# The first batch of a Fourier-mixing and gated-MLP kernel: another row order, another cut of its first stage, another layout of its spills

## The chip, the cores and the metric

The kernel runs on one core of one Trainium2 chip. The metric is the device time of one launch in microseconds, from the first instruction to the last. The kernel before takes 1937.45 us (median of 3 runs, 1937.38 to 1937.58). TensorE (PE) runs the matmuls, from tiles of up to 128 partitions in SBUF into tiles of 512 float32 values per partition in PSUM (a "bank" in the code). VectorE (DVE), ScalarE (ACT) and GpSimd (POOL) do the rest. Transfers run on 16 DMA engines and are issued here from two queues, SyncE's (SP) and ScalarE's.

## The reference

```python
def _attn_ref(x):                       # x: 8 batches x 3008 rows x 256, float32
    X = np.fft.fft(x, axis=1)
    X = np.fft.fft(X, axis=2)
    return X.real.astype(np.float32)

def _moe_ref(x, w_in, w_out):           # x: 24064 x 256, w_in 256 x 2048, w_out 2048 x 256
    h = x @ w_in
    g = h * (1.0 / (1.0 + np.exp(-1.702 * h)))
    return (g @ w_out).astype(np.float32)

out = _moe_ref(_attn_ref(x).reshape(24064, 256), w_in, w_out)
```

The kernel works in float32. It writes the 3008-point transform as 47 x 64: row s of a batch is 64 p + j. A first stage sums over the 47 values of p, for each j, with a matrix of sines and cosines; a second stage sums over j. By symmetry, j and 64 - j are taken together, and so are columns d and 256 - d (the "fold"). The weights arrive as 64-bit words and are turned into float32 by a chain of bit operations ("rounding", in 4 pieces each of w_in and w_out).

## The kernel before

Only the start of the program is touched, and the spill of every batch. The first batch is loaded into `xt` with the rows of j = 0 to 31 on partitions 0 to 46 and those of 64 - j on partitions 47 to 93, so that one matmul over 94 partitions (128 with zeros) sums both; the later batches come by `load_x`, another way, which is not touched.

```python
NA, NB = 47, 64
NJ = NB // 2
NM = 48
ENDS = 0, NJ, NJ + 1, NJ + 2
PIECES = (0, 32), (32, NA)
NU, NG = 2, 12

    ...

    def load_first(lo, hi, engines):
        for p0, p1 in PIECES:
            n, src = p1 - p0, NB * p0 * D
            engines[0].dma_start(out=xt[p0:p1, lo:hi, :].rearrange("p j d -> p (j d)"),
                                 in_=view(x, src + lo * D, [NB * D, n], [1, (hi - lo) * D]))
            t, a = xt[NA + p0:NA + p1], max(lo, 1)
            if lo == 0:
                engines[1].dma_start(out=t[:, 0, :], in_=view(x, src + NJ * D, [NB * D, n], [1, D]))
            engines[1].dma_start(out=t[:, a:hi, :], in_=view(x, src + (NB - a) * D, [NB * D, n], [-D, hi - a], [1, D]))

    def fold_first(k):
        t, e = xt[0:2 * NA, 4 * k:4 * k + 4, :], room[k % 4][0:2 * NA]
        nc.scalar.copy(free(e, 0, [D, 4], [H, 2]), free(t, 0, [D, 4], [H, 2]))
        for at, op in ((1, ALU.add), (H + 1, ALU.subtract)):
            nc.vector.tensor_tensor(e[:, :, at:at + H - 1], t[:, :, 1:H], free(t, D - 1, [D, 4], [-1, H - 1]), op=op)

    def mix_first(k):
        ps, e = bank("ps1"), room[k % 4]
        for r in range(2):
            for even in range(2):
                for c in range(2):
                    jj, (c0, c1) = 4 * k + 2 * r + c, (0, H + 1) if even else (H + 1, D)
                    w, n = (w0o, jj) if jj and not even else (w0, jj or ENDS[1 - even])
                    nc.tensor.matmul(ps[64 * c:64 * c + 64, r * D + c0:r * D + c1], lhsT=mat(w, n, slice(0, 128)),
                                     rhs=e[:, 2 * r + c, c0:c1], start=True, stop=True)
        nc.scalar.copy(xt[:, 2 * k:2 * k + 2, :].rearrange("p j d -> p (j d)"), ps[:])

    def warm(n):
        ps = bank("warm")
        for _ in range(n):
            nc.tensor.matmul(ps[:], lhsT=wcs[0][:, 0:128], rhs=wcs[0][:, 0:512], start=True, stop=True)

    def spill(b, q0=0, q1=16, engines=(nc.sync, nc.sync)):
        for c, eng in enumerate(engines):
            eng.dma_start(out=view(Td[b], (2 * q0 + c) * D, [NJ * D, NM], [2 * D, q1 - q0], [1, D]),
                          in_=xt[64 * c:64 * c + NM, q0:q1, :])

    def fill(b, a0=0, a1=NG):
        if a0 == 0:
            t4t[b] = tp.tile([128, NG, D], F32, tag="t4", name="t4")
        nc.sync.dma_start(out=t4t[b][:, a0:a1, :], in_=Td[b].rearrange("(a p) d -> p a d", p=128)[:, a0:a1, :])

    def rotate(b, a0=0, a1=NG, copy=None):
        col = t4t[b][:, a0:a1, H]
        ps = bank("psr")
        nc.tensor.matmul(ps[:, 0:a1 - a0], lhsT=rot, rhs=col, start=True, stop=True)
        (copy or nc.vector.tensor_copy)(col, ps[:, 0:a1 - a0])

    ...

    def bounds(key, low=None):
        hi, lo = raw[key][:, :, 1].bitcast(F32), raw[key][:, :, 0]
        g = sp.tile([128, 1024], F32, tag="s", bufs=3, name="g")
        m = cv.tile([128, 1024], F32, tag="m", name="m")
        r = cv.tile([128, 1024], U32, tag="r", bufs=2, name="r")
        nc.scalar.activation(g[:], hi, ACTF.Square)
        nc.gpsimd.tensor_scalar(m[:], hi, scalar1=TOP, scalar2=-TOP, op0=ALU.min, op1=ALU.max)
        ...                                  # (a variant that nothing calls)
        else:
            nc.scalar.activation(r[:].bitcast(F32), lo, ACTF.Copy, scale=2.0 ** -29, bias=2.0 ** 23)
            nc.scalar.activation(r[:], r[:].bitcast(F32), ACTF.Copy, bias=-2.0 ** 23)
        pre[key] = g, m, r

    def rounded(outs, key):
        raw.pop(key)
        g, m, r = pre.pop(key)
        ...
        dve.scalar_tensor_tensor(m[:], g[:], LOW * LOW, m[:], op0=ALU.is_ge, op1=ALU.mult)
        dve.tensor_scalar(a[:], bits, scalar1=3, scalar2=0x3FFFFFF8, op0=ALU.logical_shift_left, op1=ALU.bitwise_and)
        dve.scalar_tensor_tensor(a[:], bits, 0xC0000000, a[:], op0=ALU.bitwise_and, op1=ALU.bitwise_or)
        def finish():
            for out, part in outs(a[:], r[:]):
                nc.gpsimd.tensor_tensor(out.bitcast(U32), *part, op=ALU.add)
        return finish

    ...

    def fold_w(n):
        for cs in range(2):
            ps = bank("psw")
            for i in range(2):
                nc.tensor.matmul(ps[:], lhsT=cd[:, i, cs, :], rhs=wst[n][:, i, :], start=(i == 0), stop=(i == 1))
            nc.scalar.copy(wcs[cs][:, n * 512:(n + 1) * 512].rearrange("p (f c) -> p f c", f=4),
                           free(ps[:], 0, [1, 4], [4, 128]))
        row = cv.tile([1, 512], F32, tag="e", name="row")
        nc.scalar.activation(row[:], ps[0:1, :], ACTF.Copy, scale=2.0)
        nc.scalar.dma_start(out=af2[:, 4 * n:4 * n + 4], in_=row[:])

    ... (program order of the start; the loop over the steps of all batches follows)

    n0 = (NJ + 1) * NM + 64 - NM
    w0 = wt[:].rearrange("p a q n -> p (a q n)")[:, 0:n0 + 1]
    w0o = wt[:].rearrange("p a q n -> p (a q n)")[:, 2048:2048 + n0]
    room += [hp.tile([128, 4, D], F32, tag="h", name="e") for _ in range(4)]
    nc.vector.memset(wcs[0][:, 0:512], 1.0)
    for e in room:
        nc.gpsimd.memset(e[64:128], 0.0)
    nc.vector.memset(ones[:], 1.0)
    nc.scalar.dma_start(out=w0, in_=tab1[:, 0:n0 + 1])
    both = nc.sync, nc.scalar
    load_first(0, 8, (nc.sync, nc.sync))
    load_first(8, 20, both)
    load_first(20, 32, both)
    nc.scalar.dma_start(out=small[:], in_=tab2)
    load_in(0, nc.sync)
    load_in(1, nc.sync)
    load_out(0, nc.sync)
    warm(6)
    nc.vector.tensor_scalar(w0o, w0[:, 0:n0], scalar1=w0[:, n0:n0 + 1], scalar2=None, op0=ALU.mult)
    fold_first(0)
    for k in range(8):
        if k < 7:
            fold_first(k + 1)
        mix_first(k)
        if k in (3, 5, 7):
            spill(0, 0 if k == 3 else 2 * k - 2, 2 * k + 2, both if k == 7 else (nc.sync, nc.sync))
    fill(0, 0, 4)
    bounds(("in", 0))
    round_in(0)
    finish_in(0)
    warm(4)
    bounds(("in", 1))
    fold_w(0)
    fill(0, 4, NG)
    load_out(1, nc.sync)
    rotate(0, 0, 4, nc.scalar.copy)
    stage2(0, 0)
    round_in(1)
    finish_in(1)
    bounds(("out", 0))
    load_in(2, nc.sync)
```

So each group k of the first stage takes four values of j (`xt[:, 4k:4k+4]`), folds their rows with one ScalarE copy and two VectorE operations into `e`, runs 8 matmuls in pairs (the two `c` write different halves of the output's partitions) into one PSUM bank, and copies that bank back to `xt`. `spill` writes the result to device memory, `fill` reads it back in another order, `rotate` and `stage2` (32 matmuls of 64 x 32 each way, and a VectorE transpose) follow. Every matmul in float32 is two records in the trace. `fold_w` multiplies a rounded piece of w_in with a matrix; `hidden`, the step's first matmuls (pa and pb in the trace, L422), needs both this and stage 2. After that the program is a loop of 384 steps over all batches, with the remaining rounding of the weights among its first.

## Time and profile before

| what | value |
|---|---|
| time | 1937.45 us |
| span of the profiled execution | 1934.7 us |
| TensorE busy | 1903.0 us of it (98%) |
| VectorE, ScalarE, GpSimd busy | 1405.5, 673.3, 761.0 us |
| mean DMA rate | 53 GB/s |
| TensorE busy in the first 31 us, the next 8, the next 10.3 | 18.77, 3.59, 7.79 us (warm-up matmuls included) |
| TensorE busy from 90 to 1900 us | 1810.00 of 1810 us |

The page gives busy time of each engine as a share of the span. TensorE is busy almost throughout, and the idle time it has lies at the start and in the last microseconds. So the time is the length of the start, up to where the matmul stream begins, plus that stream. Which of the waits at the start ends last is read from the chain of waits and the timeline, not from the shares. "PEclk" in the tables of windows is the clock that TensorE was granted, 1.00 being the full one.

### The profile page before, as it was taken

How to read it: one execution, taken by the hardware profiler on the slowest of the kernel's cores; microseconds unless marked ns; L12 is line 12 of the kernel's file. 1: busy time of each engine (PE TensorE's matmuls, PEld its weight loads, DVE VectorE, ACT ScalarE, POOL GpSimd, SP SyncE). 2: the span in 40 equal slices, each digit the busy share in tenths (PEclk: the TensorE clock that was granted, in tenths of full speed). 3: DMA queues.
4: the chain of work that ended last, by engine and by line, in shares of the span. 5: the costliest groups of instructions: out<-in, count | busy, mean ns of one | idle time of the engine just before them, and what ended most of it. 6: DMA issues, size and time to landing. Idle time of an engine off the chain costs nothing.

```text
span 1934.7 us, 29225 instructions
## 1 busy us (share of the span) xinstructions
PE 1903.0 (98%) x10690; PEld 1667.3 (86%) x10690; DVE 1405.5 (73%) x2924; ACT 673.3 (35%) x927; POOL 761.0 (39%) x1049
## 2 busy tenths in 40 slices
PE   6899999999999999999999999999999999999998
PEld 3598888988889888898889888898888988889887
DVE  3877777777778677876777677777777777777776
ACT  3733333333333333333333333333333333333332
POOL 2565323643246322462235523255323643223222
PEclk8999999999999999999999999999999999999999
DMA  9630460227203362025422162221720213202201
GB/s 249 168 70 11 94 80 12 49 54 113 17 12 59 49 108 18 21 49 97 61 25 49 29 106 39 25 49 43 115 25 13 18 45 59 17 12 27 17 12 22
DMA packets 157652, 103.40 MB, mean 53 GB/s; under 512 B 105403, under 2 KB 142011, under 8 KB 156857
## 3 DMA queue, kind: packets, MB, share of 16 engines
q1 hardware_dynamic: 154160, 98.70, 30.4%
q10 hardware_dynamic: 3350, 2.84, 0.7%
q8 instruction: 85, 1.39, 0.3%
q14 instruction: 57, 0.47, 0.1%
HBM read 58.24 MB, written 48.01 MB: 55 GB/s over the span
## 4 chain that ended last, share of the span: by engine, by line
PE 96%; DMA 1%; POOL 1%; issue 1%; DVE 1%; ACT 0%; ACTq 0%; SPq 0%; DVEq 0%; POOLq 0%
PE po L489 59%; PE pa L422 17%; PE pb L422 17%; PE ps L205 1%; PE ps L287 1%; DMA xt<-in_x_dram 1%; PE psw L392 1%; PE ps L244 0%; POOL wo L354 0%; PE ps L209 0%; POOL wst L354 0%; POOL m L330 0%; DVE a L350 0%; DVE m L347 0%; DVE os L506 0%
## 5 line engine op out<-in xcount | busy, mean ns | idle before, releaser
L463 POOL TENSOR_TENSOR s<-h 128x256 f32<-128x256 f32 (+1 forms) x376 | 270.3, 719 | 1092.0 <-ACT h L451 1027.6
L489 PE MATMUL po<-s,wt 128*128 128x256 f32 (+1 forms) x2256 | 599.7, 375 | 0.0
L426 ACT COPY v<-pa 128x512 f32<-128x512 f32 (+1 forms) x384 | 222.0, 578 | 1061.8 <-PE pa L422 1061.8
L436 DVE TENSOR_TENSOR h<-v,pb 128x512 f32<-128x512 f32 (+1 forms) x384 | 259.0, 675 | 401.5 <-PE pb L422 398.7
L489 PEld LDWEIGHTS po<-s,wt 128*128 128x128 f32 x2256 | 428.6, 190 | 48.4
L489 PE MATMUL po<-h,wo 128*128 128x256 f32 (+1 forms) x1632 | 469.7, 375 | 0.5 <-ACT h L451 0.5
L451 ACT ACTIVATE h<-h 128x1024 f32<-128x1024 f32 (+1 forms) x384 | 400.8, 1044 | 18.9 <-DVE h L446 16.7
L422 PE MATMUL pa<-pq,wcs 128*128 128x256 f32 (+1 forms) x1536 | 393.7, 379 | 1.3 <-DVE pq L293 1.3
L422 PE MATMUL pb<-pq,wcs 128*128 128x256 f32 (+1 forms) x1536 | 387.9, 375 | 2.2 <-DVE dif L439 1.6
L489 PEld LDWEIGHTS po<-h,wo 128*128 128x128 f32 x1632 | 309.9, 190 | 36.4 <-issue 0.8
L422 PEld LDWEIGHTS pa<-pq,wcs 128*128 128x128 f32 x1536 | 286.8, 190 | 49.6 <-issue 11.2
L439 DVE SCALAR_TENSOR_TENSOR dif<-nb,af,pb 128x256 f32<-128x256 f32 (+1 forms) x768 | 328.3, 469 | 1.7 <-DMA af<-row 1.7
L422 PEld LDWEIGHTS pb<-pq,wcs 128*128 128x128 f32 x1536 | 291.5, 190 | 36.4 <-DVE dif L439 2.0
L464 POOL TENSOR_TENSOR s<-h 128x256 f32<-128x256 f32 (+1 forms) x376 | 276.9, 736 | 0.0
L446 DVE TENSOR_TENSOR h<-pa,dif 128x512 f32<-128x512 f32 (+1 forms) x448 | 265.4, 604 | 13.2
L489 PE MATMUL po<-h,wt 128*128 128x256 f32 (+1 forms) x752 | 220.3, 375 | 0.0
L489 PE MATMUL po<-s,wo 128*128 128x256 f32 (+1 forms) x752 | 220.3, 375 | 0.0
L467 DVE TENSOR_TENSOR s<-h,s 128x256 f32<-128x256 f32 (+1 forms) x376 | 201.2, 535 | 12.9
L466 DVE TENSOR_TENSOR s<-s,h 128x256 f32<-128x256 f32 (+1 forms) x376 | 179.5, 477 | 4.3 <-POOL s L463 4.3
L489 PEld LDWEIGHTS po<-h,wt 128*128 128x128 f32 x752 | 142.9, 190 | 16.1
L489 PEld LDWEIGHTS po<-s,wo 128*128 128x128 f32 x752 | 142.9, 190 | 16.1
L191 POOL TENSOR_TENSOR xt<-xt 111x510 f32<-111x510 f32 x56 | 74.1, 1323 | 4.4
(60 smaller groups left out, 691.8 us busy)
## 6 DMA issues: line engine op xcount, KB each, us to landing
out_dram<-os SPq DMA_DIRECT2D x284, 64.0 KB
Td<-xt SPq DMA_DIRECT2D x14, 768.0 KB
t<-Td SPq DMA_DIRECT2D x7, 1536.0 KB
xt<-in_x_dram SPq DMA_DIRECT2D x14, 512.0 KB
xt<-Xr SPq DMA_DIRECT2D x14, 512.0 KB
nb<-pq SPq DMA_DIRECT2D x23, 256.0 KB
out_dram<-os SPq DMA_DIRECT2D x96, 56.0 KB
Xr<-in_x_dram SPq DMA_DIRECT2D x7, 752.0 KB
```

Of the source, the lines that this page charges most:

```text
L191: eng.tensor_tensor(low, low, free(t, up + D - 1, [-D, 2], [-1, D - 1]), op=ALU.add)
L422: nc.tensor.matmul(ps[:, i * 256:i * 256 + n], lhsT=wcs[cs][:, f * 128:(f + 1) * 128], rhs=pq[:, cs, ks], start=True, stop=True)
L426: nc.scalar.copy(two(v[:], n), two(pa[:], n))
L436: nc.vector.tensor_tensor(two(h[:], n), two(v[:], n), two(pb[:], n), op=ALU.add)
L439: nc.vector.scalar_tensor_tensor(dif[:, i * 256:i * 256 + n], nb[:, ks], af2[:, f:f + 1], pb[:, i * 256:i * 256 + n], op0=ALU.mult, op1=AL ...
L446: nc.vector.tensor_tensor(free(h[:], 512 + at + m - 1, [256, 2], [RUN, blocks], [-1, m]), *ins, op=ALU.add)
L451: nc.scalar.activation(g, g, ACTF.Gelu_apprx_sigmoid)
L463: eng.tensor_tensor(s1, a21, a22, op=ALU.add)
L464: eng.tensor_tensor(s3, a11, a21, op=ALU.subtract)
L466: eng.tensor_tensor(s2, s1, a11, op=ALU.subtract)
L467: eng.tensor_tensor(s4, a12, s2, op=ALU.subtract)
L489: nc.tensor.matmul(pot[q][:, i, :n], lhsT=lhs, rhs=rhs, start=(p == 0 and i == 0 and f == 0), stop=(p == NP - 1), skip_group_check=True)
```

## The change

The first batch is laid out by halves: partitions 0 to 63 hold the rows of j = 0 to 31 in their natural order, partitions 64 to 127 the rows of j = 32 to 63, again in natural order, no longer reversed. Each half is loaded as rows 0 to 31 and rows 15 to 46, 32 partitions each (rows 15 to 31 twice; the matrix has zeros for the second copy). A partition then receives one contiguous run of 8 KB per load, where the reversed rows came in runs of 1 KB. As 64 - j now lies in another slot than j, the two halves can't be summed in one matmul: each product is taken over 64 partitions, and the halves are added in PSUM. Groups k and 7 - k are computed together, in two phases, so that at any time the lower half of the array adds to one bank and the upper half to the other. Between the phases two ScalarE copies of one column hold the second phase back until the first is through. The matmuls double in number and use a quarter of the array each. The columns of the second stage are permuted in the tables, so that a spill writes long runs: 16 KB per partition for the later batches, 4 KB and 2 KB for the first, against 1 KB. The order of the loads, the number of warm-up matmuls, the place of one weight load (`load_out(0)`) and the engines of a few early operations change too (cuts are marked "...", empty lines left out).

```diff
--- before.py
+++ after.py
@@ -71,13 +71,17 @@
     e0, o0, e1, o1 = ENDS
     w1[:, e0, :, 0], w1[:, o0, :, 0], w1[:, e1, :, 1], w1[:, o1, :, 1] = cos[:, 0], sin[:, 0], cos[:, NJ], sin[:, NJ]
-    w0 = np.zeros((128, NJ + 1, NG * NU, 2))
-    w0[:NA], up = w1[:, :NJ + 1], w0[NA:2 * NA]
+    up = np.zeros_like(w1[:, :NJ + 1])
     up[:, 1:NJ, :, 0], up[:, 1:NJ, :, 1] = cos[:, :NJ:-1], -sin[:, :NJ:-1]
     up[:, e0, :, 1], up[:, o0, :, 1] = cos[:, NJ], sin[:, NJ]
-    sign = np.where((np.arange(128) < NA) | (np.arange(128) >= 2 * NA), 1.0, -1.0)
-    j, k2 = np.arange(NJ)[:, None], np.arange(NB)[None, :]
+    w0 = np.zeros((2, 64, NJ + 1, NG * NU, 2))
+    for half, w in enumerate((w1[:, :NJ + 1], up)):
+        w0[half, :32], w0[half, 64 - (NA - 32):] = w[:32], w[32:]
+    sign = np.repeat([1.0, -1.0], 64)
+    c, q = np.divmod(np.arange(NJ), 16)
+    j, k2 = (4 * (q // 2) + 2 * (q % 2) + c)[:, None], np.arange(NB)[None, :]
     beta = 2.0 * np.pi * ((j * k2) % NB) / NB
     m2 = np.zeros((NU, 2, NJ, 2, NB))
     rot = np.zeros((NU, 2, NJ, NU, 2, NJ))
@@ -145,6 +149,7 @@
     def bank(name):
         return psm.tile([128, 512], F32, tag="mm", name=name)
@@ -214,36 +219,52 @@
-    room = []
+    room = {}
     def load_first(lo, hi, engines):
-        for p0, p1 in PIECES:
-            n, src = p1 - p0, NB * p0 * D
-            engines[0].dma_start(out=xt[p0:p1, lo:hi, :].rearrange("p j d -> p (j d)"),
-                                 in_=view(x, src + lo * D, [NB * D, n], [1, (hi - lo) * D]))
-            t, a = xt[NA + p0:NA + p1], max(lo, 1)
-            if lo == 0:
-                engines[1].dma_start(out=t[:, 0, :], in_=view(x, src + NJ * D, [NB * D, n], [1, D]))
-            engines[1].dma_start(out=t[:, a:hi, :], in_=view(x, src + (NB - a) * D, [NB * D, n], [-D, hi - a], [1, D]))
-    def fold_first(k):
-        t, e = xt[0:2 * NA, 4 * k:4 * k + 4, :], room[k % 4][0:2 * NA]
+        for half in range(2):
+            for g in range(2):
+                eng, p = engines[2 * half + g], 64 * half + 32 * g
+                eng.dma_start(out=xt[p:p + 32, lo:hi, :].rearrange("p j d -> p (j d)"),
+                              in_=view(x, (NB * (NA - 32) * g + NJ * half + lo) * D, [NB * D, 32], [1, (hi - lo) * D]))
+    def fold_first(g):
+        t, e = xt[:, 4 * g:4 * g + 4, :], room[g]
         nc.scalar.copy(free(e, 0, [D, 4], [H, 2]), free(t, 0, [D, 4], [H, 2]))
         for at, op in ((1, ALU.add), (H + 1, ALU.subtract)):
             nc.vector.tensor_tensor(e[:, :, at:at + H - 1], t[:, :, 1:H], free(t, D - 1, [D, 4], [-1, H - 1]), op=op)
     def mix_first(k):
-        ps, e = bank("ps1"), room[k % 4]
-        for r in range(2):
-            for even in range(2):
-                for c in range(2):
-                    jj, (c0, c1) = 4 * k + 2 * r + c, (0, H + 1) if even else (H + 1, D)
-                    w, n = (w0o, jj) if jj and not even else (w0, jj or ENDS[1 - even])
-                    nc.tensor.matmul(ps[64 * c:64 * c + 64, r * D + c0:r * D + c1], lhsT=mat(w, n, slice(0, 128)),
-                                     rhs=e[:, 2 * r + c, c0:c1], start=True, stop=True)
-        nc.scalar.copy(xt[:, 2 * k:2 * k + 2, :].rearrange("p j d -> p (j d)"), ps[:])
+        ks = k, 7 - k
+        ps = [bank("ps1") for _ in ks]
+        for phase in range(2):
+            if phase:
+                for n in range(2):
+                    nc.scalar.copy(af2[:, n:n + 1], ps[n][:, D + n * (H + 1):D + n * (H + 1) + 1])
+            for at in range(4)[::-1 if phase else 1]:
+                r, even = divmod(at, 2)
+                for half in (phase, 1 - phase):
+                    n = half ^ phase
+                    for c in range(2):
+                        jj = 4 * ks[n] + 2 * r + c
+                        c0, c1 = (0, H + 1) if even ^ half ^ phase else (H + 1, D)
+                        slot, first = ((NB - jj) % NJ if half else jj), c0 == 0
+                        w, m = (w0o, jj) if jj and not first else (w0, jj or ENDS[1 - first])
+                        rows_ = slice(64 * half, 64 * half + 64)
+                        nc.tensor.matmul(ps[n][64 * c:64 * c + 64, r * D + c0:r * D + c1], lhsT=mat(w, m, rows_),
+                                         rhs=room[slot // 4][rows_, slot % 4, c0:c1], start=(phase == 0 and at == 0),
+                                         stop=(phase == 1), skip_group_check=True)
+        for n in range(2):
+            to = placed(ks[n])
+            nc.scalar.copy(xt[:, to:to + 2, :].rearrange("p j d -> p (j d)"), ps[n][:])
+    def placed(k):
+        return 2 * k if k < 4 else 16 + 2 * k
     def load_matrices():
         for r in range(2):
@@ -256,11 +277,17 @@
         for _ in range(n):
             nc.tensor.matmul(ps[:], lhsT=wcs[0][:, 0:128], rhs=wcs[0][:, 0:512], start=True, stop=True)
-    def spill(b, q0=0, q1=16, engines=(nc.sync, nc.sync)):
+    def spill(b, ks=None, engines=(nc.sync, nc.sync)):
         for c, eng in enumerate(engines):
-            eng.dma_start(out=view(Td[b], (2 * q0 + c) * D, [NJ * D, NM], [2 * D, q1 - q0], [1, D]),
-                          in_=xt[64 * c:64 * c + NM, q0:q1, :])
+            src, at = xt[64 * c:64 * c + NM], 16 * c * D
+            if ks is None:
+                eng.dma_start(out=view(Td[b], at, [NJ * D, NM], [1, 16 * D]),
+                              in_=src[:, 0:16, :].rearrange("p q d -> p (q d)"))
+                continue
+            (k0, n), k1 = ks, 8 - sum(ks)
+            eng.dma_start(out=view(Td[b], at + 2 * k0 * D, [NJ * D, NM], [2 * (k1 - k0) * D, 2], [1, 2 * n * D]),
+                          in_=free(src, placed(k0) * D, [(placed(k1) - placed(k0)) * D, 2], [1, 2 * n * D]))
     def fill(b, a0=0, a1=NG):
         if a0 == 0:
@@ -319,22 +346,21 @@
     pre = {}
-    def bounds(key, low=None):
+    def bounds(key, first=False):
         hi, lo = raw[key][:, :, 1].bitcast(F32), raw[key][:, :, 0]
         g = sp.tile([128, 1024], F32, tag="s", bufs=3, name="g")
         m = cv.tile([128, 1024], F32, tag="m", name="m")
         r = cv.tile([128, 1024], U32, tag="r", bufs=2, name="r")
-        nc.scalar.activation(g[:], hi, ACTF.Square)
+        if first:
+            nc.vector.tensor_tensor(g[:], hi, hi, op=ALU.mult)
+        else:
+            nc.scalar.activation(g[:], hi, ACTF.Square)
         nc.gpsimd.tensor_scalar(m[:], hi, scalar1=TOP, scalar2=-TOP, op0=ALU.min, op1=ALU.max)
...
+        nc.scalar.activation(r[:].bitcast(F32), lo, ACTF.Copy, scale=2.0 ** -29, bias=2.0 ** 23)
+        nc.scalar.activation(r[:], r[:].bitcast(F32), ACTF.Copy, bias=-2.0 ** 23)
         pre[key] = g, m, r
     def rounded(outs, key):
@@ -553,31 +579,34 @@
     n0 = (NJ + 1) * NM + 64 - NM
     w0 = wt[:].rearrange("p a q n -> p (a q n)")[:, 0:n0 + 1]
     w0o = wt[:].rearrange("p a q n -> p (a q n)")[:, 2048:2048 + n0]
-    room += [hp.tile([128, 4, D], F32, tag="h", name="e") for _ in range(4)]
+    first = tp.tile([128, NG, D], F32, tag="t4", name="first")
+    rooms = [first[:, 4 * i:4 * i + 4, :] for i in range(3)]
+    rooms += [hp.tile([128, 4, D], F32, tag="h", name="e")[:] for _ in range(4)]
+    rooms += [pqp.tile([128, 4, D], F32, tag="pq", name="e")[:]]
+    room.update(zip((0, 7, 1, 6, 2, 5, 3, 4), rooms))
     nc.vector.memset(wcs[0][:, 0:512], 1.0)
-    for e in room:
-        nc.gpsimd.memset(e[64:128], 0.0)
     nc.vector.memset(ones[:], 1.0)
     nc.scalar.dma_start(out=w0, in_=tab1[:, 0:n0 + 1])
-    both = nc.sync, nc.scalar
-    load_first(0, 8, (nc.sync, nc.sync))
-    load_first(8, 20, both)
-    load_first(20, 32, both)
-    nc.scalar.dma_start(out=small[:], in_=tab2)
+    load_first(0, 8, (nc.sync,) * 4)
+    load_first(24, 32, (nc.scalar, nc.scalar, nc.sync, nc.sync))
+    load_first(8, 16, (nc.sync,) * 4)
+    load_first(16, 24, (nc.sync,) * 4)
+    nc.sync.dma_start(out=small[:], in_=tab2)
     load_in(0, nc.sync)
     load_in(1, nc.sync)
+    warm(7)
+    nc.scalar.copy(af2[0:1, 0:1], ones[0:1, 0:1])
+    nc.scalar.activation(w0o, w0[:, 0:n0], ACTF.Copy, scale=w0[:, n0:n0 + 1])
+    for k, need in enumerate(((0, 7, 1), (6, 2), (5, 3), (4,))):
+        for g in need:
+            fold_first(g)
+        mix_first(k)
+        if k:
+            spill(0, ((0, 2), (2, 1), (3, 1))[k - 1], (nc.sync, nc.scalar if k == 3 else nc.sync))
+    fill(0, 0, 4)
     load_out(0, nc.sync)
-    warm(6)
-    nc.vector.tensor_scalar(w0o, w0[:, 0:n0], scalar1=w0[:, n0:n0 + 1], scalar2=None, op0=ALU.mult)
-    fold_first(0)
-    for k in range(8):
-        if k < 7:
-            fold_first(k + 1)
-        mix_first(k)
-        if k in (3, 5, 7):
-            spill(0, 0 if k == 3 else 2 * k - 2, 2 * k + 2, both if k == 7 else (nc.sync, nc.sync))
-    fill(0, 0, 4)
-    bounds(("in", 0))
+    bounds(("in", 0), True)
     round_in(0)
     finish_in(0)
     warm(4)
```

## The prediction

> **What bounds the kernel now.** I read the totals first, then a table of windows, then the chain of waits from the first instruction to the first step. Totals:

> ```profile
> PE 1903.0 (98%) x10690; PEld 1667.3 (86%) x10690; DVE 1405.5 (73%) x2924; ACT 673.3 (35%) x927; POOL 761.0 (39%) x1049
> ```

> TensorE has some 32 us of idle time. Windows (start:end, length, busy us and count per engine, granted clock, share of the DMA engines, GB/s) say where:

> ```profile
> 0.00:31.00 31.00, 18.77 (x141) 13.53 (x142) 11.41 (x19) 6.32 (x17) 6.26 (x9) 0.83 0.99 224
> 31.00:39.00 8.00, 3.59 (x8) 1.32 (x8) 3.15 (x3) 6.92 (x7) 2.40 (x2) 0.92 0.78 261
> 39.00:49.30 10.30, 7.79 (x74) 3.67 (x74) 1.13 (x4) 3.75 (x6) 1.02 (x1) 0.73 0.92 328
> 90.00:1900.00 1810.00, 1810.00 (x10213) 1601.19 (x10212) 1335.57 (x2813) 618.63 (x853) 721.09 (x1014) 1.00 0.29 46
> ```

> From 90 to 1900 us TensorE never waits, so 16 KB runs for the later spills, which run beside it, can gain nothing there. The first 90 us decide. The chain of waits (start, duration, what):

> ```profile
> 11.88 10.33 DMA xt<-in_x_dram
> ...
> 23.01 0.69 DVE e L234
> 23.70 0.14 issue
> 23.83 7.14 PE ps L244 x96
> 30.97 0.02 issue
> 31.00 0.59 ACT xt L246
> ...
> 31.98 1.16 ACT g L329
> ...
> 36.60 2.36 POOL wst L354
> 38.96 0.04 issue
> 39.01 6.42 PE psw L392 x8
> ```

> The reader sees loads of x until 22, the first stage to 31.59, then the rounding of the first weight piece (ScalarE's square, three VectorE operations, GpSimd's addition) to 38.96, then its matmuls (fold_w). They end at 45.43, and the first step's matmuls start at 49.34. The way through device memory (spill, fill) lies beside this: the fill is issued at 38.73. So the end moves by what the rounding's end moves, if the fill keeps up.

> Two more things matter. First, what a load costs:

> ```profile
> 8.00:16.00 8.00, 1.58 (x4) 0.38 (x2) 0.27 (x1) 0.00 (x0) 0.00 (x0) 0.86 1.16 170
> 42.00:45.00 3.00, 3.00 (x5) 1.21 (x5) 0.00 (x0) 0.59 (x1) 0.00 (x0) 0.58 1.10 364
> 83.00:86.00 3.00, 3.00 (x16) 2.64 (x15) 2.86 (x3) 2.71 (x3) 0.12 (x1) 1.00 1.05 201
> 87.00:90.00 3.00, 3.00 (x9) 1.34 (x8) 2.78 (x4) 0.61 (x2) 3.00 (x3) 1.00 1.09 108
> ```

> At 42 to 45 runs the fill: 128 partitions, 1 KB runs, 364 GB/s. At 83 to 90 run the loads of batch 1, 2 KB runs: by order of issue 32 partitions first (201 GB/s), then 15 (108). The engines are fully taken in all four. So partitions, not run length, set the rate: reversed 1 KB rows weren't what made x slow. Second, the clock:

> ```profile
> 13.50:14.00 0.50, 0.00 (x0) 0.00 (x0) 0.00 (x0) 0.00 (x0) 0.00 (x0) 0.77 1.22 191
> 14.00:14.50 0.50, 0.00 (x0) 0.00 (x0) 0.00 (x0) 0.00 (x0) 0.00 (x0) 0.50 1.09 113
> 20.50:21.00 0.50, 0.45 (x7) 0.20 (x4) 0.00 (x0) 0.00 (x0) 0.00 (x0) 0.90 0.66 94
> 24.00:24.50 0.50, 0.50 (x8) 0.50 (x7) 0.50 (x2) 0.00 (x0) 0.00 (x0) 0.51 0.84 98
> ```

> It falls to half at about 13.8, returns at 20.6 and falls again at 24.0, though the second gap was only 2.9 us.

> [...]

> **Part 1, the loads.** Before: 3.08 MB of x and 0.82 MB of matrix; the half-microsecond windows show 98 GB/s at 24.0, 410 at 25.5, so x is in by about 25.4. After: 16 loads of 0.262 MB, 4.19 MB in all, plus 0.82, is 5.01 MB. By 7.2, when the matrix lands (the wait of L571), 1.45 MB are through before; I keep that. The other 3.56 MB at 200 to 218 GB/s take 16.3 to 17.8 us: all in at 23.5 to 25.0, and I take 24.5 with the landing. Counting back 1.05 MB / 0.205 = 5.1 us per set of slots: slots 24 to 31 at 14.3, 8 to 15 at 19.4. A third more bytes eats what the loss of the 15-partition loads saves.

> **Part 2, the first stage.** A fold is two VectorE operations of 0.677 us (row L234), 1.36. Matmuls before: 32 records in 3.47 us at half clock are 8 pairs at 0.43; full clock 0.22. After: per pair of groups 32 matmuls in 8 sets of four quarters, two phases of 4 sets; the array time is the same if the quarters overlap. A phase is 0.87 us, or 1.73 at half clock; between them two ScalarE copies of a column, 0.17 each (row L275): a pair of groups takes 2.1 or 3.8. Then two evacuations of 0.59, nearly end to end: 1.1; and the next fold's ScalarE copies, 0.2 each, stand behind them in program order.
> The first pair needs slots 24 to 31 and two folds: 17.1, cold (warm-ups end near 10.4), to 20.9. Second: 22.4 to 24.5. The third needs the last load and two folds (group 5, then 3): 24.5 + 2.7 = 27.2, to 29.3 (full) or 31.0. Evacuation and copy 1.3; fourth pair 2.1, or some 3.0 partly cold: 32.7 or 35.3; evacuation: **33.8 or 36.4**, against 31.59. This part loses 2.2 to 4.8 us: fold, matmul, evacuation now follow the last load twice in a row.

> **Part 3, the rounding.** Before 31.59 to 39.01: 7.4 us. After: the square is on VectorE, and the VectorE and GpSimd work is done beside the first stage. Data of w_in at 24.5 + 1.0 (tab2) + 2.6 = 28.1, GpSimd 2.45, VectorE 1.24 + 0.69 + 1.23: 33.8, before ScalarE's two operations (1.15 + 1.06) after the last evacuation: 36.0 or 38.6. Then GpSimd 2.36: fold_w starts at **38.5 or 41.1**. Gain of this part 2.7.

> **Part 4, the clock in fold_w.** Before 6.42 us, nearly all at half clock. After: in the first case a gap of about 4 us, a coin's toss, 4.9 on average; in the second under 3 us, 3.4. End 43.4 or 44.5 against 45.43: gain 0.9 to 2.0.

> **Part 5, transfers later.** The three spills (1.57 MB at about 200 GB/s, after the w_in pieces) end near 38, the fill lands near 41.5: hidden under fold_w. But w_out's piece 0 (1.05 MB, 2.7 us) now stands behind the fill and pushes w_in's piece 2, which had 2.6 us to spare (transfers over at 50.3, used at 52.9): some 0.6 to 1 us given back.
> Sum of the central estimates: -1.5 + 0.8, about **-0.7 us**; with weight on the first rival, **-1.9**: 1935.6.

> **Rivals.** (1) Halves overlap on the two queues (slots 24 to 31 are split so), or 8 KB runs load faster: x in by 19. Then VectorE and ScalarE's loop (about 3.7 us per pair) bound the stage, it ends near 27, and the gain is 5 to 7: about 1931. For it: the seven warm-ups end at 10.4, which makes sense only if the first pair follows soon. Against: 170 and 201 GB/s. (2) Every pair runs cold, and the piece of w_in is late too: fold_w starts 3 us later, 1939 to 1940. For it: a 2.9 us gap was enough at 24.0. (3) Shorter start, same end: the rounding chain of the later pieces and its loads set the stream's start, 1937.4. For it: GpSimd and its pieces lead the chain from 52 to 78 us; against: each of them follows the first in program order, so it moves along.

> **Range and chances.** The first rival gives the low end, 1931.5, the second the high end, 1939.0. Nothing after 90 us can move by 39 us: within 2% 0.98, 0.01 on each side.

> **What would show it.** Right: all of x in at 23 to 26, near 200 GB/s from 8 to 24; the third pair waiting for VectorE behind the last load; the last evacuation at 33 to 37 with fold_w less than 5 us after it; a first step 0 to 3 us earlier. Wrong: x in by 20, the first stage over before 30 (rival 1); quarters that don't overlap (a phase over 1.2 us at full clock); fold_w waiting for the fill; TensorE gaps between 90 and 1900.

## The result, and the profile after

The changed kernel takes **1940.17 us** (median of 4 runs, 1939.85 to 1940.27), the kernel before beside it 1937.41 (4 runs, 1937.14 to 1937.58): ratio 1.0014, 95% interval 0.9997 to 1.0031. Twelve more runs (the experiment after_again) put the ratio at 1.0011, interval 1.0003 to 1.0020: slower, by about 2 us. The prediction said 1935.6.

One thing is needed to read all that follows. In the profile of the changed kernel TensorE's granted clock falls from 1.00 to 0.50 at 12.01, 39.31, 49.55, 70.03 and 83.69 us, which are 8, 3, 6 and 4 times 3.41 us apart; the first fall lasts four such stretches (to 25.66), the others one each (to 42.73, 52.97, 73.45 and 87.10). The changes seen in the other traces, too, lie whole stretches of 3.41 us apart; I call them windows. They lie elsewhere in other executions (the first fall of the same kernel comes at 11.29 us in after_again), and one and the same kernel varies by up to 4 us to either side (the kernel before from 1934.01 to 1941.61 us, in the 189 runs that stand beside the experiments). Time and clock go together: over these 189 runs, time and mean clock have a correlation of -0.85, some 0.7 us for each 0.001 of clock. So I give, beside each ratio, the difference of the means to the kernel before of the same batch, with its standard error; for the changed kernel it is **+2.25 +- 0.49 us** (after_again), and every experiment is held against that. The four batches ran on different chips, so comparisons across them go by way of the kernel before, whose means there are 1937.58 to 1938.08.

The totals of the page of the changed kernel, and its table of windows:

```profile
PE 1910.3 (99%) x10820; PEld 1671.9 (86%) x10820; DVE 1407.8 (73%) x2924; ACT 674.1 (35%) x936; POOL 755.5 (39%) x1045
```

```profile
0.00:31.00 31.00, 20.22 (x213) 12.94 (x213) 11.76 (x19) 8.31 (x23) 2.15 (x5) 0.78 0.96 261
...
49.30:90.00 40.70, 35.73 (x118) 24.20 (x118) 33.21 (x45) 28.81 (x34) 22.41 (x15) 0.87 0.69 192
90.00:1900.00 1810.00, 1810.00 (x10206) 1600.61 (x10205) 1335.27 (x2810) 617.46 (x853) 718.58 (x1012) 1.00 0.30 46
```

The same stretch from 49.3 to 90 us before:

```profile
49.30:90.00 40.70, 34.41 (x126) 22.87 (x127) 34.32 (x45) 30.02 (x37) 23.20 (x15) 1.00 0.68 178
```

TensorE is still busy without a gap from 90 us on. The new thing is between 49 and 90: a mean clock of 0.87 instead of 1.00, and 118 matmul records done instead of 126. The loss of this pair of profiles (spans 1937.9 and 1934.7) begins there, after the point to which the prediction worked its sum. The chain of waits of the changed kernel (start, duration, what):

```profile
33.35 1.08 ACT xt L264 x2
...
36.04 1.07 ACT r L363
...
37.18 2.38 POOL wst L380
...
39.60 5.25 PE psw L418 x8
...
69.64 5.41 PE psw L418 x8
...
76.17 6.14 DMA af<-row
...
83.25 1.69 PE pb L448 x4
```

Against the lines shown of before: the last evacuation ends at 34.43 (31.59), the rounding ends at 39.6 (39.0), fold_w ends at 44.85 (45.43), and the first step starts at 49.09 (49.34). That is within what the prediction said would happen. But the third fold_w (69.64) runs cold, 5.41 us where it took 3.70 before, and a 2 KB transfer behind it, `af<-row`, takes 6.14 us. The end of this stretch before:

```profile
81.08 0.79 DVE dif L439 x2
...
81.92 1.13 PE pb L422 x4
```

The first matmuls of step 0, before and then after:

```profile
49.34 1.13 PE L422 MATMUL pa<-pq,wcs 128*128 128x256 f32 x4 [1.25 <-DVE pq L293]
49.09 1.66 PE L448 MATMUL pa<-pq,wcs 128*128 128x256 f32 x4 [1.25 <-DVE pq L320]
```

The second matmuls (pb) of step 5 (the sixth step, as they are counted from 0; an expectation below calls it the fifth) start at 81.92 before and 83.25 after. From the first step's start that is 32.58 us before, 34.16 after. They then run cold too, 1.69 us for 1.13, and from their start to the end of the span it is 1852.7 us before and 1854.7 after. So the two spans differ by -0.25 + 1.58 + 1.94 = 3.3 us.

### The profile page after: what moved, and what is told of

It reads as the page before. It is cut to its first block, busy times and chain, and to the rows that moved or that the text cites. A ratio compares the mean times of both kernels' runs of the same rounds, so it can differ in the third digit from the quotient of the medians.

```text
span 1937.9 us, 29491 instructions
## 1 busy us (share of the span) xinstructions
PE 1910.3 (99%) x10820; PEld 1671.9 (86%) x10820; DVE 1407.8 (73%) x2924; ACT 674.1 (35%) x936; POOL 755.5 (39%) x1045
## 4 chain that ended last, share of the span: by engine, by line
PE 96%; DMA 2%; POOL 1%; issue 0%; DVE 0%; ACT 0%; ACTq 0%; POOLq 0%
PE po L515 59%; PE pa L448 17%; PE pb L448 17%; PE ps L210 1%; PE ps L314 1%; DMA xt<-in_x_dram 1%; PE psw L418 1%; DMA raw<-in_moe_w_in_dram 1%; POOL wst L380 0%; DMA af<-row 0%; PE ps L214 0%; POOL wo L380 0%; POOL m L360 0%; PE ps L259 0%; ACT xt L264 0%
## 5 line engine op out<-in xcount | busy, mean ns | idle before, releaser
L448 PEld LDWEIGHTS pb<-pq,wcs 128*128 128x128 f32 x1536 | 292.4, 191 | 36.4 <-DVE dif L465 2.3
L320 DVE STREAM_TRANSPOSE pq<-ps 128x256 f32<-128x256 f32 x96 | 34.6, 417 | 57.3 <-PE ps L314 57.3
```

What stands on the lines that cost most here:

```text
L320: nc.vector.transpose(free(pq[:], cs * 512 + u * RUN, [256, 2], [NU * RUN, 4], [1, RUN]), free(ps[u][:], cs * 256, [128, 2], [32, 4], [1, ...
L448: nc.tensor.matmul(ps[:, i * 256:i * 256 + n], lhsT=wcs[cs][:, f * 128:(f + 1) * 128], rhs=pq[:, cs, ks], start=True, stop=True)
```

## The experiments

The theory after these two profiles, **A**: TensorE's clock. The changed first stage is sparse, a gap behind every pair of groups, and a window mostly taken up by gaps is followed by half the clock (TensorE was busy 22% and 45% of the windows ahead of the falls at 70.0 and 83.7). Rivals: **B**, the order of transfers (the moved weight load makes `af<-row` late); **C**, the layout itself adds work and waits at any clock.

| kernel | ratio, 95% interval | means, us from before | mean clock |
|---|---|---|---|
| after_again | 1.0011, 1.0003 to 1.0020 | +2.25 +- 0.49 | 0.9918 |
| after_later | 1.0019, 1.0011 to 1.0026 | +3.57 +- 0.43 | 0.9924 |
| before_later | 1.0012, 1.0004 to 1.0019 | +1.94 +- 0.40 | 0.9933 |
| after_filled | 1.0062, 1.0047 to 1.0077 | +11.90 +- 1.10 | 0.9922 |
| after_busy | 1.0006, 0.9998 to 1.0015 | +0.97 +- 0.31 | 0.9965 |
| before_busy | 0.9988, 0.9979 to 0.9996 | -2.52 +- 0.31 | 0.9980 |
| after_out0_early | 1.0004, 0.9997 to 1.0011 | +0.89 +- 0.46 | 0.9931 |
| before_runs | 1.0000, 0.9991 to 1.0008 | -0.23 +- 0.41 | 0.9944 |
| after_busy2 | 0.9996, 0.9987 to 1.0004 | -0.81 +- 0.62 | 0.9975 |
| after_wide | 0.9989, 0.9982 to 0.9996 | -2.12 +- 0.47 | 0.9938 |
| before_square | 0.9986, 0.9979 to 0.9992 | -2.97 +- 0.28 | 0.9946 |
| before_square_busy | 0.9987, 0.9979 to 0.9995 | -2.71 +- 0.43 | 0.9974 |
| after_square_back | 1.0022, 1.0013 to 1.0030 | +4.07 +- 0.38 | 0.9932 |
| after_ahead | 0.9997, 0.9989 to 1.0005 | -0.69 +- 0.38 | 0.9945 |
| after_busy2_out0 | 0.9991, 0.9983 to 0.9999 | -1.27 +- 0.38 | 0.9975 |
| after_best | 0.9981, 0.9974 to 0.9989 | -3.52 +- 0.30 | 0.9985 |

The kernel before has a mean clock of 0.9937 to 0.9942 in these batches.

### Is it the place of the windows? after_again, after_later, before_later

after_again is the changed kernel unchanged. The later ones hold the loads back by two GpSimd fills of tiles that the first transfers write:

```diff
     nc.vector.memset(ones[:], 1.0)
+    nc.gpsimd.memset(xt[:, 0:7, :], 0.0)
+    nc.gpsimd.memset(w0[:, 0:1], 0.0)
     nc.scalar.dma_start(out=w0, in_=tab1[:, 0:n0 + 1])
```

(before_later has the same two lines, with the clearing of `e` moved behind them.)

> The changed kernel once more. Theory A (clock windows): the 3 us lost against the kernel before are lost after the first step has begun[...]; if their place is a matter of the kernel, this run shows the drops at 49.6, 70.1 and 83.7 us again and 1940.2 us; if it is a matter of the run, the drops and the time differ (1937 to 1940). Theory B (transfers): the later loads and the slow transfer of the small vector cost it; then 1940.2 whatever the place of the windows.

> The changed kernel with its first loads held back by about 1.7 us (a memset that they must wait for). Theory A: if the windows stay where they are, the gap before the third fold_w moves from 67.0-69.6 to 68.7-71.3 and is cut by the window's edge near 70.0, so no drop there; 1.7 us later and 3 us won: about 1938.9. Theory B: 1.7 us longer, 1941.9.

> The kernel before with its first loads held back by about 1.7 us in the same way. Theory A: the gap before the third fold_w moves from 67.1-69.8 to 68.8-71.5, inside the window 68.4-71.8, so the clock drops for one window at least: 1937.4 + 1.7 + 1.5 to 3, that is 1940.6 to 1942. Theory B: 1.7 us longer, 1939.1.

Measured: +2.25, +3.57 and +1.94. The delay costs the two kernels 1.3 and 1.9 us (fold_w starts 1.3 and 2.3 us later in their traces), no more than its own length. A in its first form, that the time hangs on where the program stands in fixed windows, missed both (1938.9 expected and 1941.15 measured, 1940.6 to 1942 expected and 1939.52 measured); B's figures, which count the delay alone, came nearer. In after_again's own trace the clock falls at 11.3, 69.3 and 83.0 us, in the first profile of the same kernel at 12.0, 39.3, 49.6, 70.0 and 83.7. The place of the windows is a matter of the execution. What a kernel has of its own is how many gaps it offers them, and how long they are.

Three windows show what a gap does. From the changed kernel, 3.41 us up to the falls at 70.0 and 83.7:

```profile
66.61:70.03 3.42, 0.75 (x3) 0.30 (x2) 3.18 (x5) 2.58 (x4) 2.97 (x2) 1.00 0.45 137
80.27:83.68 3.41, 1.54 (x9) 1.06 (x8) 2.01 (x4) 3.41 (x5) 2.67 (x2) 1.00 0.21 45
```

From the kernel before, its window on the gap ahead of the third fold_w:

```profile
68.39:71.80 3.41, 1.98 (x5) 1.02 (x6) 3.23 (x5) 2.56 (x3) 1.38 (x1) 1.00 1.02 335
```

Both kernels have a gap of 2.67 us ahead of the third fold_w. After, nearly all of it lay in one window (TensorE busy 0.75 of 3.42 us, 22%), and the clock fell; before, 1.98 us were busy (58%), and it stayed. The gap being the same, this fall comes of where the window lay in these two executions, and it needs no new layout: in the trace of before_busy (below) the third fold_w runs cold too. The gap ahead of step 5's pb is longer after the change, 1.87 us against 1.57; there a window with 1.54 us busy (45%) let the clock fall.

### Fillers: after_filled, after_busy, before_busy, after_busy2

Matmuls on data that nobody reads are put into the gaps. after_filled put 6 ahead of the third fold_w and 3 into step 5:

```diff
+            for _ in range(6 if (n, cs) == (2, 0) else 0):
+                nc.tensor.matmul(ps[:], lhsT=wcs[0][:, 0:128], rhs=wcs[0][:, 0:512], start=True, stop=True)
...
+            for _ in range(3 if (t, cs) == (5, 1) else 0):
+                nc.tensor.matmul(psr_tile[0][:, 8:512], lhsT=wcs[0][:, 0:128], rhs=wcs[0][:, 0:504], start=True, stop=True)
```

> The changed kernel with TensorE kept busy in two gaps: six extra 128x512 matmuls (2.6 us at full clock) into the bank of the third fold_w ahead of it, and three (1.3 us) between pa and pb of step 5, into unused columns; their results are overwritten or never read. Theory A: no drop at 70.1 and 83.7, fold_w(2) 3.5 us instead of 5.4: about 1937.1 (3 us won). Theory B: 1940.2 or somewhat more for the extra work.

At +11.90, where A expected 3 us less, it tells nothing of the theories: I had taken 0.43 us for a filler, but a float32 matmul of 128x512 is two records, 0.85 us at full clock and 1.7 at half, and the second set waited 5.59 us for a VectorE copy of the bank it wrote. One thing in its trace counts: there the clock stayed at half from 12.0 to 39.3 us, through the whole first stage, and the first fold_w started at 43.02 instead of 39.60.

The others fill the first stage, into a bank of their own. In the changed kernel (after_busy; after_busy2 has 15, then 2, 3, 1, then 6):

```diff
+        if not idle:
+            idle.append(pso.tile([128, 512], F32, tag="o0", name="warm"))
-        ps = bank("warm")
+        ps = idle[0]
...
-    warm(7)
+    warm(13)
...
         mix_first(k)
+        warm((2, 4, 1, 0)[k])
...
-    warm(4)
+    warm(7)
```

before_busy: 14 for 6 at the start, 4 behind group 1, 9 for 4 ahead of fold_w.

> The changed kernel with more warm-up matmuls (0.85 us each at full clock, into a bank that is free until the loop): 13 instead of 7 at the start, 2, 4 and 1 after the first three pairs of groups, 7 instead of 4 before the first fold_w, so that TensorE has no long gap until then. Theory A, second form: executions differ by where the clock's windows fall, and the changed kernel is slower on average because its first stage leaves TensorE idle about half of the time and so at half clock for longer (mean clock 0.992 against 0.994). Then this kernel gains 2 to 4 us on the changed one (mean 1939.9): 1936 to 1938, mean clock 0.995 or more. Theory B (transfers) or C (the chain fold, matmul, copy is longer at any clock): 1939 to 1940.

> The kernel before with its gaps filled the same way: 14 warm-up matmuls instead of 6 at the start, 4 after group 1, 9 instead of 4 before the first fold_w. Theory A: the first fold_w takes 3.4 us instead of 6.4, and groups 2 to 7 run at full clock: 2 to 4 us less than the kernel before (mean 1937.6): 1934 to 1936. If the difference of the two filled kernels is under 1 us, the layout itself costs nothing at equal clock; if it stays at 2 us, theory C. Theory B: no change, 1937.5.

> The changed kernel with more filler matmuls, sized at 0.85 us each so that no pair of groups waits for them: 15 ahead of the first pair, 2, 3 and 1 behind the first three, 6 ahead of the first fold_w. Theory A (the loss is TensorE's clock[...]): mean clock over 0.996, fold_w starts by 40 and its 8 matmuls take 3.7 us, time 1937 to 1938.5. Theory C (the new layout costs the same at any clock, by the work added): the clock rises all the same, but the time stays at 1939 or above.

after_busy: +0.97, a mean of 1939.05, which misses A's 1936 to 1938 and lies where B and C expected it; the clock rose, but the fillers pushed the pairs, and fold_w started at 41.81. after_busy2, better sized: **-0.81, 3.1 us less than the changed kernel** (3.06 +- 0.79), at a clock of 0.9975. Theory A said 1937 to 1938.5, and the mean was 1937.22; C said 1939 or more. before_busy shows that the kernel before had the same fault, though in a denser stage: -2.52. In the trace of after_busy2, which is of the fastest of its 13 runs, the first fold_w starts at 38.80 and takes 3.70 us.

But the fillers take about as much from either kernel (3.1 and 2.5 us), so the clock of the first stage is a loss of both and hardly tells them apart. Filled, at nearly one clock (0.9975 and 0.9980), the kernels still differ by 1.71 +- 0.69 us, and with the square on VectorE in both (before_square_busy, below) by 1.90 +- 0.75. By the expectation of before_busy that speaks for C, and it is near the 2.2 us that the prediction's part 2 put as the loss of the new first stage at full clock. Of this, 1.1 us stand at fold_w (after_busy2, then before_square_busy):

```profile
38.80 3.70 PE L422 MATMUL psw<-wst,small 128*128 128x512 f32 x8 [0.78 <-POOL wst L384]
37.72 3.70 PE L399 MATMUL psw<-wst,small 128*128 128x512 f32 x8 [1.41 <-POOL wst L361]
```

### Order of transfers: after_out0_early

```diff
     load_in(1, nc.sync)
+    load_out(0, nc.sync)
...
     fill(0, 0, 4)
-    load_out(0, nc.sync)
```

> The changed kernel with the load of w_out's first piece back where it was, before the first stage, so that it no longer stands behind the fill. Theory B: the later pieces of the weights arrive 2.7 us earlier and 1 to 2 us are won: 1938 to 1939. Theory A: the spills now wait behind 1.05 MB more (2.7 us), the fill is late by some 2 us but lies beside fold_w: 1939.9 or up to 1 us more.

Measured +0.89, 1.36 +- 0.67 less than the changed kernel: B is likely, and not certain from the times. In its trace the gap ahead of step 5's pb is 1.11 us, against 1.87 and 1.92 in the changed kernel and after_again, and no fall follows it. The mechanism is in the timelines of the two queues. After:

```profile
75.25 0.35 SPq L175 DMA_DIRECT2D xt<-in_x_dram  x1
76.17 0.48 ACTq L425 DMA_DIRECT2D af<-row  x1
```

Before:

```profile
74.65 0.48 ACTq L399 DMA_DIRECT2D af<-row  x1
79.56 0.34 SPq L170 DMA_DIRECT2D xt<-in_x_dram  x1
```

Before, the load of batch 1 waits for the small transfer (the queue's waits name `af<-row`, 4.8 us) and goes out behind it. With the weight load moved, the same load waits for something else, goes out at 75.25, and the small transfer lands behind it at 82.31. The chain runs through `af<-row` (6.05 to 6.18 us) in the traces of the changed kernel, after_again and after_later; it does not in after_out0_early, where the load goes out at 80.36, nor in those with a warm third fold_w (after_ahead, after_busy2), where the small transfer is issued a little ahead of the load. This suggests that A and B are linked, a cold fold_w making the small transfer late enough to meet the load. It is not shown: in after_square_back the third fold_w is cold as well (5.41 us) and the small transfer goes out behind the load (80.99 and 79.88), yet the chain does not run through it.

### Parts alone: before_runs, before_square, after_square_back, before_square_busy

before_runs is the kernel before with only the spills in long runs and the tables permuted for them:

```diff
-    j, k2 = np.arange(NJ)[:, None], np.arange(NB)[None, :]
+    c, q = np.divmod(np.arange(NJ), 16)
+    j, k2 = (4 * (q // 2) + 2 * (q % 2) + c)[:, None], np.arange(NB)[None, :]
...
-            eng.dma_start(out=view(Td[b], (2 * q0 + c) * D, [NJ * D, NM], [2 * D, q1 - q0], [1, D]),
-                          in_=xt[64 * c:64 * c + NM, q0:q1, :])
+            eng.dma_start(out=view(Td[b], (16 * c + q0) * D, [NJ * D, NM], [1, (q1 - q0) * D]),
+                          in_=xt[64 * c:64 * c + NM, q0:q1, :].rearrange("p q d -> p (q d)"))
```

> The kernel before with only the permuted columns of the second stage and the spills in long runs (16 KB for later batches; 8 KB and 4 KB for the first). All theories: after 90 us nothing waits for it, and the first batch's spill lies beside the rounding: 1937.5, within 0.5 us. If it is faster or slower by 1 us or more, the spills matter where no wait shows it.

before_square is the kernel before with the square of the first piece on VectorE (`nc.vector.tensor_tensor(g[:], hi, hi, op=ALU.mult)`); after_square_back undoes this in the changed kernel (`bounds(("in", 0))`); before_square_busy is before_square with fillers (14; 4 behind group 1; 6).

> The kernel before with one thing of the change: the square of the first w_in piece on VectorE instead of ScalarE. The prediction's part 3 puts the change's gain there: fold_w starts 2 to 2.7 us sooner (36.5 instead of 39.0), 1935 to 1936. If the gain came of the earlier weight loads instead, or if the stream waits for the later pieces (rival 3): 1937.4.

> The changed kernel with the one helpful part undone: the square of the first w_in piece back on ScalarE, behind the last evacuation. Before_square showed this part alone to be worth 3.0 us (means 1935.06 against 1938.03). If it is worth the same in the changed kernel, as the account needs: fold_w starts 1 to 2.5 us later than 39.6 and the mean goes from 1939.9 to 1941.5 to 1943. If the first stage's other losses already hide it: 1939.9.

> The kernel before with the square on VectorE and with the filler matmuls of before_busy (14 at the start, 4 behind group 1, 6 ahead of fold_w). If the two gains add: 1933 to 1934, faster than both kernels. If they take the same wait away: 1935.4, as before_busy alone.

The long runs: nothing (-0.23). The square: **-2.97**, and the chain of before_square shows where:

```profile
34.30 2.37 POOL wst L357
...
36.72 5.41 PE psw L395 x8
```

fold_w starts 2.3 us sooner than at 39.01. Undone in the changed kernel it costs 1.82 +- 0.62 (+4.07 against +2.25): helpful there too, though the size is uncertain. So without the square, the change loses 4 us. The square and the fillers together give -2.71, not -5.5: the mean of 1935.32 is the second of the two cases expected (1935.4), in which both take the same wait away. In that trace fold_w (37.72, 3.70 us) is done early, and stage 2 then waits 1.76 us for the fill from device memory, which lands at 43.2; there the path beside has become the longer one.

### Loads, and the loop behind them: after_wide, after_ahead

after_wide loads each set of slots by one transfer of 128 partitions. It reads other rows than the reference needs, so its output is another; bytes and everything behind are the same.

```diff
-        for half in range(2):
-            for g in range(2):
-                eng, p = engines[2 * half + g], 64 * half + 32 * g
-                ...
+        engines[0].dma_start(out=xt[:, lo:hi, :].rearrange("p j d -> p (j d)"),
+                             in_=view(x, lo * D, [16 * D, 128], [1, (hi - lo) * D]))
```

> The changed kernel with each of the four loads of x as one transfer of 128 partitions with 8 KB each instead of four of 32 partitions (the rows read are others than the reference's, so the output is another; bytes, tiles and everything behind are the same). If 32 partitions set the rate (the prediction's part 1): about 400 GB/s, x in by 14 to 17 us instead of 24, the last evacuation near 27 to 30, fold_w starts 4 to 6 us sooner, 1934 to 1937. If the 16 engines or device memory set the rate: 200 GB/s as before, 1940.

The windows of after_wide, and below them one of the changed kernel (the last column is GB/s):

```profile
12.00:14.00 2.00, 0.00 (x0) 0.00 (x0) 0.91 (x2) 0.31 (x2) 0.00 (x0) 0.60 0.98 414
18.00:20.00 2.00, 1.59 (x28) 1.35 (x22) 2.00 (x4) 0.85 (x2) 1.06 (x1) 0.70 1.03 414
```

```profile
12.00:14.00 2.00, 0.07 (x2) 0.07 (x4) 1.28 (x2) 0.21 (x1) 0.00 (x0) 0.50 0.98 209
```

Same bytes, same 8 KB per partition, and 414 GB/s instead of 209, at the same share of the DMA engines (0.98): here the rate went with the partitions of one transfer, 128 for 32. That the rows also lie 16 KB apart in device memory instead of 64 no run separates. The mean is -2.12, 4.4 us less than the changed kernel, and fold_w starts at 36.41, 3.2 us sooner (4 to 6 expected). But the last evacuation ends only at 31.25, not at 27 to 30. VectorE has folded everything by 21.5; what is left is ScalarE's loop (timeline of after_wide):

```profile
22.88 1.07 ACT L261 COPY xt<-ps 128x512 f32<-128x512 f32 x2 [1.03 <-PE ps L256]
23.84 0.33 ACT L232 COPY e<-xt 128x8 f32<-128x8 f32 x2
25.23 0.35 ACT L245 COPY af<-ps 128x1 f32<-128x1 f32 x2 [1.06 <-PE ps L256]
26.58 1.07 ACT L261 COPY xt<-ps 128x512 f32<-128x512 f32 x2 [1.01 <-PE ps L256]
```

Evacuation, fold copy, matmuls, column copy, matmuls, evacuation: 3.7 us a pair, with TensorE at work for 2.1 of it (0.93 and 1.12). after_ahead takes one link out: the folds of the next pair are issued ahead of the evacuations.

```diff
-    def mix_first(k):
+    def mix_first(k, then=()):
...
+        for g in then:
+            fold_first(g)
         for n in range(2):
             to = placed(ks[n])
...
-    for k, need in enumerate(((0, 7, 1), (6, 2), (5, 3), (4,))):
-        for g in need:
-            fold_first(g)
-        mix_first(k)
+    for g in (0, 7, 1):
+        fold_first(g)
+    for k, then in enumerate(((6, 2), (5, 3), (4,), ())):
+        mix_first(k, then)
```

> The changed kernel with each pair's folds issued ahead of the evacuations of the pair before them, so that ScalarE's column copies of group 4 no longer stand behind the third pair's evacuations. The prediction's part 2 says that fold, matmul and evacuation follow the last load twice in a row, 1.3 us of it ScalarE's: the last evacuation ends 1 to 1.5 us sooner than 33.4 to 34.4, fold_w starts by 38.5, mean 1938.5 to 1939. If something else holds the fourth pair (VectorE's fold, the clock): under 0.5 us, 1939.9.

ScalarE's timeline in the changed kernel, third pair's evacuations to the fourth's:

```profile
29.75 1.07 ACT L264 COPY xt<-ps 128x512 f32<-128x512 f32 x2 [1.01 <-PE ps L259]
30.71 0.22 ACT L235 COPY e<-xt 128x8 f32<-128x8 f32 x1
...
33.35 1.07 ACT L264 COPY xt<-ps 128x512 f32<-128x512 f32 x2 [1.01 <-PE ps L259]
```

In after_ahead:

```profile
28.54 0.21 ACT L235 COPY e<-xt 128x8 f32<-128x8 f32 x1
30.18 1.07 ACT L266 COPY xt<-ps 128x512 f32<-128x512 f32 x2 [1.43 <-PE ps L259]
...
32.65 1.07 ACT L266 COPY xt<-ps 128x512 f32<-128x512 f32 x2 [1.11 <-PE ps L259]
```

From evacuation to evacuation 2.47 us instead of 3.60: the wait was real, 1.1 us. The last evacuation ends at 33.72 instead of 34.43 and fold_w starts at 38.88 instead of 39.60, so 0.7 us arrive where 1 to 1.5 were expected. The time fell by 2.94 +- 0.62 (-0.69 against +2.25), more than that and more than expected. The clock went from 0.9918 to 0.9945 with it. In the trace fold_w itself is cold (5.40 us), and what is won lies behind the first step, where the third fold_w is warm (3.70 us) and no fall comes near 83. That the new order causes this is not shown.

### What is left: after_busy2_out0, after_best

after_busy2_out0 joins the edits of after_busy2 and after_out0_early. after_best adds those of after_ahead, with fillers (2, 3, 0, 0) between the pairs.

> The changed kernel with the fillers of after_busy2 and the weight load back in its old place. Theory A plus B (clock and order of transfers are two separate losses): after_busy2's mean of 1937.2 falls by about 0.9 to 1936.3, and the gap ahead of the fifth step's second matmuls goes from 1.85 to 1.1 to 1.6 us. If B's gain in after_out0_early was chance: 1937.2 and the gap stays.

> All three repairs of the changed kernel together: fillers, the weight load in its old place, the folds ahead of the evacuations. If the losses are separate and add: 1935 to 1935.5, no worse than the kernel before with the square alone (mean 1935.06), so that the layout itself costs nothing more. If the layout has a further cost: 1936.5 or above.

-1.27: 0.46 +- 0.73 less than after_busy2, too little to tell. The gap ahead of step 5's pb went from 1.85 to 1.57 us. after_best: **-3.52, 1934.25 us median, ratio 0.9981 (0.9974 to 0.9989)**, faster than both kernels, 5.8 +- 0.6 us below the changed one. It is also 2.26 +- 0.48 us below after_busy2_out0, at 0.001 more clock (0.7 us by the slope above): most of what the new order of the folds brings here is not the clock. So of C there was this, a wait in the program order of the new first stage, and not the layout as such. after_best isn't told apart from before_square (-2.97 +- 0.28), which has the old layout and one changed instruction. So with its gaps closed the new layout costs nothing that these runs can see, and nothing shows that it brings anything.

## Why the prediction was wrong, point by point

- **Part 1, loads: right.** All of x in at 24.24 us (24.5 said), near 209 to 234 GB/s from 10 to 24. That partitions and not run length set the rate was tested by after_wide: 414 GB/s with 128 partitions and the same 8 KB.
- **Part 2, first stage: right.** Last evacuation at 34.43 (33.8 or 36.4 said), a warm pair's phases 0.94 and 1.12 us, so the quarters overlap. That fold, matmul and evacuation follow the last load twice was confirmed by after_ahead.
- **Part 3, rounding: right.** fold_w at 39.60 (38.5 or 41.1). The gain of this part, put at 2.7, was 2.2: between 34.43 and 39.60 are 5.2 us (a sign of being right was less than 5), 7.4 before. The square alone brought fold_w forward by 2.29 and the time by 2.97.
- **Part 4, clock in fold_w: right in kind, a coin's toss as said.** 5.25 us in one profile, 3.70 in after_again; the chance itself was an estimate, and two traces don't measure it. The first step came 0.25 and 1.8 us sooner than before's 49.34.
- **Part 5, later transfers: wrong transfer.** I looked for bytes that push w_in's piece 2. The chain shows a 2 KB transfer behind the next batch's load instead; the load of w_out in its old place gave back 1.36 +- 0.67 us.
- **The step that failed** is the reason given against rival 3: "each of them follows the first in program order, so it moves along". From it I carried a gain at the first step unchanged to the end. GpSimd's pieces do move along: before_square's fold_w is 2.29 us sooner, and step 5's pb 3.24. But between the first step and step 5's pb the changed kernel takes 34.16 us (34.24 in after_again) where the kernel before takes 32.58: a cold third fold_w, then the late transfer. From there to the end it takes 1854.7 us in both traces, where the kernel before takes 1852.7, for the clock falls once more, at 83.7 and 83.0. A start that is 0.25 or 1.8 us earlier is lost in this.
  Behind the step stands a premise, that the clock is a toss inside fold_w only. In the traces of both layouts (after_filled left out) half clock comes behind gaps as late as 83.7 us, and the stretch takes 32.6 us where TensorE has the full clock from 50 us on (the four of the kernel before without fillers, after_ahead, after_busy2, after_busy2_out0) and 33.8 to 35.5 in the ten where half clock comes into it behind 50, 33.96 in before_busy and 34.95 in before_square_busy among them. I read the clock of one profile, which has no fall behind 37.7, as the kernel's; that was luck, and the sum lacks a term for half clock over many executions. How much oftener the changed kernel is hit is seen only in the mean clocks, 0.9918 against 0.9942, which by the slope above are some 1.7 us.
- **Rivals.** Rival 1 (x in by 19) fell at the loads. But its "about 3.7 us per pair" is exactly the loop seen in after_wide. Rival 2, every pair cold, is what the trace of after_filled shows (fold_w at 43.02); 1939 to 1940 came, though mostly by the losses behind the first step. I had taken it as one outcome of small weight, where it is a share of the executions and so a part of the mean.

What stays open: how the 5.8 us that after_best recovers divide. The three repairs alone give 3.1, 2.9 and 1.4, each with an error of 0.6 to 0.8, so that not even an overlap is certain. Open too is why the new order of the folds alone gave four times the 0.7 us that fold_w gained.

## What to carry to other kernels

A gain at the head of a chain is only worth what the next ten waits leave of it: follow the chain to the point from which the bottleneck never idles again, and give every gap on that engine up to there its own chance of a lower clock (here it fell behind one of 1.87 us, as late as 83.7 us). Before rearranging data, try the cheap part alone; here one instruction moved to another engine gained about as much as all the repairs together (-2.97 +- 0.28 and -3.52 +- 0.30 us). And when loads look slow, count the partitions of one transfer before the length of its runs: here 128 for 32, with the same 8 KB each, went with 414 GB/s for 209.
